# Zero-padded QK matmuls in 128x32 tiles, and an output projection spread over eight steps, in an attention + SwiGLU block

## The chip, the cores and the metric

The kernel runs on one core of one Trainium2 chip. The metric is the device time of one execution in microseconds (us), and the table values are medians of several executions. Executions of one kernel agreed within about 0.6%. A ratio is computed as the mean time of one kernel's runs over the mean time of the other's runs of the same rounds, so it is not quite the ratio of the medians quoted beside it. "The profile" is one traced execution.

Names used below: PE is TensorE's matmul row, PEld its weight loads, ACT is ScalarE, DVE is VectorE, POOL is GpSimd, SP is SyncE. A *pass* is 512 columns streamed through the array; matmuls that sit in different tiles of the array and stream together share a pass. A *key tile* is 128 keys; a *step* is one query chunk of 512 tokens and one group of four heads, and has 16 key tiles. Attention has 32 steps, so 512 key tiles.

## The reference

S = 2048 tokens, D = 1024, 32 heads of 32 with one shared key/value head, F = 3584, bfloat16.

```python
mod = (silu(c) @ w_mod)                      # six vectors: sa, ca, ga, sb, cb, gb
h = layernorm(x) * (1 + ca) + sa
q, k, v = h @ wq, h @ wk, h @ wv             # 32 query heads, one k and one v of width 32
p = softmax(q @ k.T * 32 ** -0.5)
x = x + ga * ((p @ v) @ wo)
h = layernorm(x) * (1 + cb) + sb
x = x + gb * ((silu(h @ w1) * (h @ w3)) @ w2)
```

## The kernel before

Three stages follow each other: a front end (modulation, layer norm, q, k, v), attention with the output projection, and the MLP. The change touches mostly attention. Keys are stored transposed four times over, once in each group of 32 partitions (`kT4`), so that each of four heads can use its own 32 rows of the array. One matmul contracts over 32 rows, and two such row tiles stream side by side:

```python
def qk_pair(pair, kt, idx, qc, hg):
    rows = (0, 1) if pair == 0 else (2, 3)
    a_exp.wait(t, idx)                                   # the exp has read these two PSUM banks
    for r in rows:
        ins = t.matmul(self.bank(r), self.kT4[32 * r:32 * r + 32, kt * 128:(kt + 1) * 128],
                       self.qT8[32 * r:32 * r + 32, hg, qc * 512:(qc + 1) * 512],
                       start=True, stop=True, tile_position=(32 * r, 0))
    p_qk.inc(ins)

def pv_all(kt, idx, bpv, bden):
    a_expA.wait(t, idx + 1); a_expB.wait(t, idx + 1)
    pts = (ptA[idx % 3], ptA[idx % 3], ptB[idx % 3], ptB[idx % 3])
    for j in range(4):                                   # 128x32 column tiles, all four side by side
        t.matmul(self.bank(bpv)[32 * j:32 * (j + 1), :], self.V16[:, kt, :], pts[j][...],
                 start=(kt == 0), stop=(kt == NKT - 1), tile_position=(0, 32 * j))
    for j in range(4):                                   # the same with a block of ones: denominators
        ins = t.matmul(self.bank(bden)[32 * j:32 * (j + 1), :], self.ones_k[:, :], pts[j][...], ...)
    p_pv.inc(ins)
# ... per key tile: qk_pair(0, kt), qk_pair(1, kt), pv_all(kt - 1)
# ... only in the step with hg == 0: the projection of the previous query chunk, 64 matmuls of 128x128
```

ACT turns the scores into exps, one instruction for each pair of banks:

```python
p_qkA.wait(a, idx + 1)
a_expA.inc(a.activation(ptA[idx % 3][:], self.bank(0, 2), ACT.Exp, scale=scale))
p_qkB.wait(a, idx + 1)
a_expB.inc(a.activation(ptB[idx % 3][:], self.bank(2, 2), ACT.Exp, scale=scale))
```

At the end of a step DVE takes the reciprocal of the denominators and multiplies, both straight from PSUM; two pairs of banks alternate for PV and denominators, and the projection borrows the idle pair.

The softmax here doesn't subtract the row's maximum and nothing guards it: scores larger than these inputs give would overflow.

## Time and profile before

| | before |
|---|---|
| median | 1916.1 us (4 runs, 1915.8 to 1916.6) |
| first exp | 167.0 us |
| attention, first exp to the end of the last | 1092.0 us |
| from there to the MLP's first transpose | 30.2 us |
| MLP | 624.7 us |

The lines of the page: first the busy time of the engines as a share of the span, then rows of the 40 slices. In those rows a digit is the busy share in tenths, and in PEclk the granted share of the TensorE clock.

```profile
PE 1754.7 (92%) x9864; PEld 520.4 (27%) x9864; DVE 474.6 (25%) x698; ACT 1051.9 (55%) x1144; POOL 31.8 (2%) x43
...
PE   1797999999999999999999999969998998998999
...
ACT  0004999998988888888889999931100100110110
...
PEclk9897555558555558555567555568999999999999
```

The PE row says that PE is busy nearly everywhere. The PEclk row says that through the whole of attention this busy PE runs at half speed, apart from short rises (at 449, 722 and 995 us). At half clock a pass takes 0.43 us instead of 0.22 and counts as busy all the while, so the first row alone hides this. The Trainium skill distrusts that row for another reason: "Trainium Kernel Development and Optimization", section Performance Expectations, says that matmul busy time is a bad metric for how close a kernel is to the hardware's limit because matmuls are pipelined. It does not name the clock; here the row misleads because of the clock (97% busy at clock 0.50 in the first window below).

The windows view, three stretches: attention without projection, attention with it, and MLP. Columns are the stretch, its length, then busy us and number of instructions for each engine, the granted clock, the DMA share and GB/s.

```profile
core 0: us, PE busy (x) PEld busy (x) DVE busy (x) ACT busy (x) POOL busy (x), PEclk, DMA share, GB/s
205.00:405.00 200.00, 194.25 (x1142) 32.67 (x1140) 21.71 (x13) 183.04 (x190) 0.00 (x0) 0.50 0.00 1
449.00:475.00 26.00, 24.45 (x192) 7.35 (x188) 5.52 (x9) 21.55 (x24) 0.00 (x0) 1.00 0.00 1
1300.00:1500.00 200.00, 194.01 (x911) 88.11 (x910) 67.76 (x102) 24.48 (x41) 8.83 (x10) 0.99 0.32 106
```

Count the exps: 190 ACT instructions in 200 us is one in 1.053 us, so about 2.1 us for a key tile (2.107 us from the steps, which take 33.71 us for 16 key tiles). The groups of instructions (operation, shapes, count, busy us, mean ns of one, idle time before it and who ended it):

```profile
L474 PE MATMUL ps<-qT,kT 32*128 32x512 bf16 x2048 | 542.3, 584 | 62.2 <-ACT ptB L461 43.5
L459 ACT ACTIVATE ptA<-ps 128x1024 bf16<-128x1024 f32 x512 | 525.3, 1026 | 115.0 <-PE ps L474 109.3
L461 ACT ACTIVATE ptB<-ps 128x1024 bf16<-128x1024 f32 x512 | 521.6, 1019 | 0.0
```

ACT waits for QK before the A exp, 109.3 us in all. The timeline shows one such loop (start, length, engine, line, operation; in brackets the idle time before it and what ended it):

```profile
350.31 1.02 ACT L459 ACTIVATE ptA<-ps 128x1024 bf16<-128x1024 f32 x1 [0.24 <-PE ps L474]
...
350.67 0.61 PE L485 MATMUL ps<-ptA,V 128*32 128x512 bf16 x2
...
351.07 0.63 PE L491 MATMUL ps<-ptA,ones_k 128*32 128x512 bf16 x2
...
351.23 1.02 ACT L461 ACTIVATE ptB<-ps 128x1024 bf16<-128x1024 f32 x1
...
351.64 1.27 PE L474 MATMUL ps<-qT,kT 32*128 32x512 bf16 x4
352.30 0.10 PEld L474 LDWEIGHTS ps<-qT,kT 32*128 32x128 bf16 x2 [0.56 <-ACT ptB L461]
352.35 1.02 ACT L459 ACTIVATE ptA<-ps 128x1024 bf16<-128x1024 f32 x1
...
352.84 0.61 PE L485 MATMUL ps<-ptA,V 128*32 128x512 bf16 x2
```

The A exp at 350.31 is followed by the B exp 0.92 us later: that is ACT's own pace (0.919 us on average over the 646 intervals below 0.96 us). The PE needs 0.40 us from PV to the denominators and 0.57 us from there to the next QK; the matmuls come back to PV after 2.17 us here, 2.107 us on average. ACT could do a key tile in 1.84 us, so PE at half clock sets the pace.

### The profile page before, as it was taken

To read this page: it belongs to the slowest core of one execution; us is meant where nothing else is said; L and a number is where in the kernel's file an instruction comes from. 1 tells how busy PE (TensorE), PEld (TensorE's weight loads), DVE (VectorE), ACT (ScalarE), POOL (GpSimd) and SP (SyncE) were. 2 spreads that over 40 slices of the span, in tenths; PEclk is the share of its full clock that TensorE was granted. 3 is DMA by queue.
4 is the path that set the end of the run, shared out by engine and by line. 5 is a ranking of instruction groups with operands and counts; after the bars stand their busy time and mean duration, and the time that the engine had idled before them with its cause. 6 is when DMAs were issued, how large, how long until landed. Compare 5 with 4: busy or idle time off the path is not lost. (4 is left out here: it accounts for less than half of the span.)

```text
span 1913.9 us, 23304 instructions
## 1 busy us (share of the span) xinstructions
PE 1754.7 (92%) x9864; PEld 520.4 (27%) x9864; DVE 474.6 (25%) x698; ACT 1051.9 (55%) x1144; POOL 31.8 (2%) x43
## 2 busy tenths in 40 slices
PE   1797999999999999999999999969998998998999
PEld 0342111112111112111121111124444444444444
DVE  5551100102501013010112101133413423332431
ACT  0004999998988888888889999931100100110110
POOL 1000000000000000000000000000000000000000
PEclk9897555558555558555567555568999999999999
DMA  9305100000000000000000000002412512421420
GB/s 319 132 1 187 56 1 1 1 1 1 1 1 1 1 1 1 1 1 1 1 1 1 1 1 1 1 1 88 154 38 96 175 56 66 165 94 61 132 89 22
DMA packets 48293, 93.30 MB, mean 49 GB/s; under 512 B 1392, under 2 KB 30064, under 8 KB 48192
## 3 DMA queue, kind: packets, MB, share of 16 engines
q1 hardware_dynamic: 39360, 57.94, 8.9%
q0 software_dynamic: 8832, 33.88, 5.2%
q8 instruction: 79, 1.29, 0.3%
q14 instruction: 22, 0.18, 0.0%
HBM read 87.62 MB, written 4.19 MB: 48 GB/s over the span
## 5 line engine op out<-in xcount | busy, mean ns | idle before, releaser
L474 PE MATMUL ps<-qT,kT 32*128 32x512 bf16 x2048 | 542.3, 584 | 62.2 <-ACT ptB L461 43.5
L459 ACT ACTIVATE ptA<-ps 128x1024 bf16<-128x1024 f32 x512 | 525.3, 1026 | 115.0 <-PE ps L474 109.3
L461 ACT ACTIVATE ptB<-ps 128x1024 bf16<-128x1024 f32 x512 | 521.6, 1019 | 0.0
L673 ACT ACTIVATE sg<-ps 128x512 bf16<-128x512 f32 x112 | 66.9, 597 | 504.1 <-PE ps L743 504.1
L579 DVE RECIPROCAL rden<-ps 128x512 f32<-128x512 f32 x32 | 107.3, 3352 | 841.6 <-PE ps L491 841.6
L491 PE MATMUL ps<-ptA,ones_k 128*32 128x512 bf16 x1024 | 313.5, 611 | 0.0
L491 PE MATMUL ps<-ptB,ones_k 128*32 128x512 bf16 x1024 | 313.5, 611 | 0.0
L485 PE MATMUL ps<-ptA,V 128*32 128x512 bf16 x1024 | 302.4, 588 | 0.8 <-ACT ptB L461 0.8
L485 PE MATMUL ps<-ptB,V 128*32 128x512 bf16 x1024 | 302.4, 588 | 0.0
L474 PEld LDWEIGHTS ps<-qT,kT 32*128 32x128 bf16 x2048 | 103.2, 98 | 661.9 <-ACT ptA L459 377.8
L743 PE MATMUL ps<-h2T,w1b 128*128 128x512 bf16 x896 | 218.0, 387 | 15.2 <-DVE h2T L695 15.2
L748 PE MATMUL ps<-h2T,w3b 128*128 128x512 bf16 x896 | 213.5, 381 | 0.0
L761 PE MATMUL ps<-w_sb,hact 128*128 128x512 bf16 x896 | 194.1, 379 | 3.4 <-DVE hact L707 3.4
L703 DVE TENSOR_TENSOR gs<-ps,sg 128x512 bf16<-128x512 f32 x112 | 77.4, 691 | 190.1 <-ACT sg L673 190.1
L743 PEld LDWEIGHTS ps<-h2T,w1b 128*128 128x128 bf16 x896 | 88.7, 99 | 124.6 <-DVE h2T L695 16.0
L748 PEld LDWEIGHTS ps<-h2T,w3b 128*128 128x128 bf16 x896 | 88.3, 99 | 107.9 <-issue 3.9
L761 PEld LDWEIGHTS ps<-w_sb,hact 128*128 128x128 bf16 x896 | 87.4, 98 | 110.1 <-DVE hact L707 5.3
L485 PEld LDWEIGHTS ps<-ptA,V 128*32 128x32 bf16 x1024 | 52.5, 100 | 215.4 <-issue 215.4
L707 DVE TENSOR_TENSOR hact<-ps,gs 128x512 bf16<-128x512 f32 x112 | 77.4, 691 | 53.9 <-PE ps L748 53.9
L459 ACT ACT_TABLE_LOAD x1 | 1.3, 1283 | 135.8 <-PEq L126 135.8
L511 PE MATMUL ps<-wo_sb,oT 128*128 128x512 bf16 x256 | 67.5, 408 | 4.3 <-DVE oT L582 4.3
L714 DVE TENSOR_TENSOR x_sb<-ps,x_sb 128x512 bf16<-128x512 f32 x32 | 22.1, 691 | 175.1 <-PE ps L761 175.1
(69 smaller groups left out, 616.4 us busy)
## 6 DMA issues: line engine op xcount, KB each, us to landing
w1b<-in_B_w_dram SPq DMA_DIRECT2D x28, 1024.0 KB, 5.3
w3b<-in_B_w_dram POOLq DMA_DIRECT2D x28, 1024.0 KB, 8.0
wmod_sb<-in_w_mod_dram SPq DMA_DIRECT2D x2, 6144.0 KB, 27.7
w_sb<-in_B_w_dram SPq DMA_DIRECT2D x1, 7168.0 KB, 29.3
x_sb<-in_A_x_dram SPq DMA_DIRECT2D x4, 1024.0 KB, 10.5
out_dram<-x_sb SPq DMA_DIRECT2D x16, 256.0 KB, 2.0
wq_sb<-in_A_wq_dram POOLq DMA_DIRECT2D x1, 2048.0 KB, 18.1
wo_sb<-in_A_wo_dram POOLq DMA_DIRECT2D x1, 2048.0 KB, 23.9
```

The costliest lines, as they stand in the source:

```text
L459: a_expA.inc(a.activation(ptA[idx % 3][:], self.bank(0, 2), ACT.Exp, scale=scale))
L461: a_expB.inc(a.activation(ptB[idx % 3][:], self.bank(2, 2), ACT.Exp, scale=scale))
L474: ins = t.matmul(self.bank(r), self.kT4[32 * r:32 * r + 32, kt * 128:(kt + 1) * 128], self.qT8[32 * r:32 * r + 32, hg, qc * 512:(qc + 1) * ...
L485: t.matmul(self.bank(bpv)[32 * j:32 * (j + 1), :], self.V16[:, kt, :], pts[j][:, jj * 512:(jj + 1) * 512], start=(kt == 0), stop=(kt == NK ...
L491: ins = t.matmul(self.bank(bden)[32 * j:32 * (j + 1), :], self.ones_k[:, :], pts[j][:, jj * 512:(jj + 1) * 512], start=(kt == 0), stop=(kt ...
L511: ins = t.matmul(self.bank(bnk), self.oT[:, hg2, j * 128:(j + 1) * 128], self.wo_sb[:, hg2, half * 512:(half + 1) * 512], start=(hg2 == 0) ...
L579: c0 = v_r.inc(v.reciprocal(self.rden[:], self.bank(bden)))
L703: v_gs.inc(v.tensor_tensor(self.gs[k][:], self.bank(4 + 2 * k), self.sg[k][:], op=ALU.mult))
L707: v_hact.inc(v.tensor_tensor(self.hact[:, fc, :], self.bank(5 + 2 * k), self.gs[k][:], op=ALU.mult))
L743: ins = t.matmul(self.bank(4 + 2 * k), self.w1b[buf][:, cch, sub * 128:(sub + 1) * 128], self.h2T[b][:, cch, :], start=(cch == 0), stop=(c ...
L748: ins = t.matmul(self.bank(5 + 2 * k), self.w3b[buf][:, cch, sub * 128:(sub + 1) * 128], self.h2T[b][:, cch, :], start=(cch == 0), stop=(c ...
L761: ins = t.matmul(self.bank(bnk), self.hact[:, fc, j * 128:(j + 1) * 128], self.w2_sb[:, fc, half * 512:(half + 1) * 512], start=(fc == 0), ...
```

## The change

The intent is to give the array more work on purpose, so that the clock gate opens (the throttle that sets PE's granted clock, in these traces always 0.50 or 1.00): QK now contracts over all 128 rows, with three quarters of the stationary operand zero, in the same 128x32 tiling that PV uses. Around it, the projection is spread over all eight steps of a query chunk, PV and denominators are copied out of PSUM early so that one pair of banks is enough, the front end's loads are reordered, and w1/w3 blocks are halved and no longer prefetched (the padded keys need the memory). The core of the diff, with cuts:

```diff
-                self.kT4 = ER12(nc.sbuf_tensor("kT4", [P, S], BF16, side="right"))
+                self.kTpad = ER12(nc.sbuf_tensor("kTpad", [P, 4, S], BF16, side="right"))
 ...  POOL zeroes it once; DVE writes head r's keys to its own 32 partitions of copy r
+                SM["g_pad"].inc(g.memset(self.kTpad[:], 0.0))
+                            ins3 = v.tensor_copy(self.kTpad[32 * r:32 * r + 32, r, qc * 512:(qc + 1) * 512],
+                                                 self.bank(BK)[32 * r:32 * r + 32, :])
 ...  QK
-                        ins = t.matmul(self.bank(r), self.kT4[32 * r:32 * r + 32, kt * 128:(kt + 1) * 128],
-                                       self.qT8[32 * r:32 * r + 32, hg, qc * 512:(qc + 1) * 512],
-                                       start=True, stop=True, tile_position=(32 * r, 0))
+                        for c in range(4):
+                            k0 = kt * 128 + 32 * c
+                            ins = t.matmul(self.bank(r)[32 * c:32 * (c + 1), :], self.kTpad[:, r, k0:k0 + 32],
+                                           self.qT8[:, hg, qc * 512:(qc + 1) * 512],
+                                           start=True, stop=True, tile_position=(0, 32 * c))
 ...  projection: 64 units of four 128x32 matmuls, eight units in each step, one per key tile
-                    op_chunks = oproj_chunks(qc - 1) if (hg == 0 and qc > 0) else []
+                    if hg == 0 and qc > 0:
+                        units = oproj_units(qc - 1)
+                    my_units = units[8 * hg:8 * hg + 8] if units else []
 ...  end of a step on DVE
-                        c0 = v_r.inc(v.reciprocal(self.rden[:], self.bank(bden)))
+                        v_evac.inc(v.tensor_copy(self.pv_sb[:], self.bank(bpv)))
+                        v_evac.inc(v.tensor_copy(self.den_sb[:], self.bank(bden)))
+                        v_evac.wait(v, v_evac.count)
+                        c0 = v_r.inc(v.reciprocal(self.rden[:], self.den_sb[:]))
 ...  front end: modulation weights before most of x; wq, wk, wv, wo released by them
-                for i in range(4):
+                d_x[0].inc(sp.dma_start(self.x_sb[:, 0:TPC, :], self.xv[:, 0:TPC, :]), 16)
+                d_wm[0].inc(sp.dma_start(wmod_sb[:], wmod_v[:, :, 0:HALF]), 16)
+                for i in range(1, 4):
                     d_x[i].inc(sp.dma_start(self.x_sb[:, i * TPC:(i + 1) * TPC, :], ...), 16)
-                d_wm[0].inc(sp.dma_start(wmod_sb[:], wmod_v[:, :, 0:HALF]), 16)
-                d_x[3].wait(g, 16)
+                d_wm[0].wait(g, 16)
 ...  MLP blocks of 256 columns, allocated after attention
-            NPRE = min(2, self.NQC * self.FB)
+            NPRE = 0
```

More of the change, by code (lines that the diff above doesn't have):

```diff
@@ L60, in __init__ @@
         DH = D // H
-        assert DH == 32 and D % P == 0 and S % 512 == 0 and F % 512 == 0
+        assert DH == 32 and D % P == 0 and S % 512 == 0 and F % 256 == 0
         assert tuple(w_mod.shape) == (D, 6 * D)
@@ L69, in __init__ @@
         self.FC = F // P
-        self.FB = F // 512
+        self.FW = 256
+        self.FPB = self.FW // P
+        self.FB = F // self.FW
         assert self.HG == self.DC
@@ L82, in build @@
                 "d_c", "d_x0", "d_x1", "d_x2", "d_x3", "d_wmod", "d_wmod2", "d_wo", "d_wqkv", "d_w2", "d_w1a", "d_w1b", "d_w3a", "d_w3b", "o_out",
-                "g_aux",
+                "g_aux", "g_pad",
                 "a_sig", "a_sd", "a_expA", "a_expB", "a_sg",
@@ L87, in build @@
                 "v_aux", "v_mod", "v_wo", "v_st", "v_xn", "v_ht", "v_kev", "v_vev", "v_qev",
-                "v_r", "v_evac", "v_res", "v_gs", "v_hact", "v_w2s",
+                "v_r", "v_evac", "v_ot", "v_res", "v_gs", "v_hact", "v_w2s",
             ]
@@ L133, in build @@
                 self.w2_sb = EL2(nc.sbuf_tensor("w2_sb", [P, FC, D], BF16))
-                self.w1b = [EL2(nc.sbuf_tensor(f"w1b{i}", [P, DC, 512], BF16)) for i in range(2)]
-                self.w3b = [EL2(nc.sbuf_tensor(f"w3b{i}", [P, DC, 512], BF16)) for i in range(2)]
                 with ExitStack() as stR2:
@@ L140, in build @@
                     self.rden = ER2(nc.sbuf_tensor("rden", [P, 512], F32, side="right"))
-                    self.oT = ER2(nc.sbuf_tensor("oT", [P, HG, 512], BF16, side="right"))
+                    self.pv_sb = ER2(nc.sbuf_tensor("pv_sb", [P, 512], F32, side="right"))
+                    self.den_sb = ER2(nc.sbuf_tensor("den_sb", [P, 512], F32, side="right"))
+                    self.oT = ER2(nc.sbuf_tensor("oT", [P, 2, HG, 512], BF16, side="right"))
                     self.phase2()
@@ L145, in build @@
                     ER3 = stR3.enter_context
+                    self.w1b = [ER3(nc.sbuf_tensor(f"w1b{i}", [P, DC, self.FW], BF16, side="right")) for i in range(2)]
+                    self.w3b = [ER3(nc.sbuf_tensor(f"w3b{i}", [P, DC, self.FW], BF16, side="right")) for i in range(2)]
                     self.xn2 = ER3(nc.sbuf_tensor("xn2", [P, 4, D], BF16, side="right"))
@@ L355, in _ @@
                     p_k.wait(v, qc + 1)
-                    v_kev.inc(v.tensor_copy(self.kT4[:, qc * 512:(qc + 1) * 512], self.bank(BK)))
                     p_v.wait(v, qc + 1)
@@ L363, in _ @@
                         v_qev.inc(v.tensor_copy(self.qT8[:, hg, qc * 512:(qc + 1) * 512], self.bank(bq)))
+                        if 2 <= hg < 6:
+                            if qc == 0 and hg == 2:
+                                SM["g_pad"].wait(v, 1)
+                            r = hg - 2
+                            ins3 = v.tensor_copy(self.kTpad[32 * r:32 * r + 32, r, qc * 512:(qc + 1) * 512],
+                                                 self.bank(BK)[32 * r:32 * r + 32, :])
+                            if r == 3:
+                                v_kev.inc(ins3)
                     if qc == 0:
@@ L428, in _ @@
                         v_kev.wait(sp, v_kev.count)
-                        o.inc(sp.dma_start(dbg["kT4"], self.kT4[:]), 16)
+                        o.inc(sp.dma_start(dbg["kT4"], self.kTpad[:]), 16)
                     if "V16" in dbg:
@@ L487, in pv_all @@
                                  start=(kt == 0), stop=(kt == NKT - 1), tile_position=(0, 32 * j))
+                    if kt == 0:
+                        v_evac.wait(t, 2 * (idx // NKT))
                     ins = None
@@ L494, in pv_all, with oproj_units @@
                     p_pv.inc(ins)
-                def oproj_chunks(qc):
-                    chunks = []
+                v_ot = SM["v_ot"]
+                def oproj_units(qc):
+                    ob = qc % 2
+                    units = []
                     for g in range(8):
@@ L500, in oproj_chunks, with emit @@
                         bnk = BOP + g % 2
-                        def grp(g=g, j=j, half=half, bnk=bnk, first=True):
-                            pass
-                        for c2 in range(2):
-                            def emit(g=g, j=j, half=half, bnk=bnk, c2=c2):
-                                if c2 == 0:
+                        for hg2 in range(HG):
+                            def emit(g=g, j=j, half=half, bnk=bnk, ob=ob, hg2=hg2):
+                                if hg2 == 0:
                                     v_res.wait(t, 8 * qc + g - 2 + 1)
@@ L507, in emit @@
                                     if g == 0:
-                                        v_evac.wait(t, (qc + 1) * HG)
+                                        v_ot.wait(t, (qc + 1) * HG)
                                 ins = None
-                                for hg2 in range(4 * c2, 4 * c2 + 4):
-                                    ins = t.matmul(self.bank(bnk), self.oT[:, hg2, j * 128:(j + 1) * 128],
+                                for cq in range(4):
+                                    ins = t.matmul(self.bank(bnk)[32 * cq:32 * (cq + 1), :],
+                                                   self.oT[:, ob, hg2, j * 128 + 32 * cq:j * 128 + 32 * (cq + 1)],
@@ L512, in emit @@
                                                    self.wo_sb[:, hg2, half * 512:(half + 1) * 512],
-                                                   start=(hg2 == 0), stop=(hg2 == HG - 1))
-                                if c2 == 1:
+                                                   start=(hg2 == 0), stop=(hg2 == HG - 1), tile_position=(0, 32 * cq))
+                                if hg2 == HG - 1:
                                     p_op.inc(ins)
-                            chunks.append(emit)
@@ L517, in oproj_chunks @@
-                    return chunks
+                            units.append(emit)
+                    return units
                 NSTEP = NQC * HG
+                bpv, bden = 4, 5
                 qk_pair(0, 0, 0, 0, 0)
                 qk_pair(1, 0, 0, 0, 0)
+                units = []
                 for step in range(NSTEP):
                     qc, hg = step // HG, step % HG
-                    s = step % 2
-                    bpv, bden = 4 + 2 * s, 5 + 2 * s
                     base = step * NKT
-                    op_chunks = oproj_chunks(qc - 1) if (hg == 0 and qc > 0) else []
@@ L528, in _ @@
-                    v_evac.wait(t, step - 1)
-                    if s == 1 and hg == 1 and qc > 0:
-                        v_res.wait(t, 8 * qc)
-                    n_op = len(op_chunks)
+                    if hg == 0 and qc > 0:
+                        units = oproj_units(qc - 1)
+                    my_units = units[8 * hg:8 * hg + 8] if units else []
+                    kt0 = 4 if NKT >= 12 else 1
+                    upk = (8 + (NKT - kt0 - 1)) // (NKT - kt0)
                     for kt in range(1, NKT):
@@ L535, in _ @@
                         qk_pair(1, kt, idx, qc, hg)
+                        if kt == 1:
+                            v_evac.wait(t, 2 * step - 1)
                         pv_all(kt - 1, idx - 1, bpv, bden)
-                        if op_chunks and kt >= 3:
-                            k_issue = 2 if len(op_chunks) > (NKT - 1 - kt) else 1
-                            for _ in range(k_issue):
-                                if op_chunks:
-                                    op_chunks.pop(0)()
+                        if kt >= kt0:
+                            for _ in range(upk):
+                                if my_units:
+                                    my_units.pop(0)()
                     if step + 1 < NSTEP:
@@ L546, in _ @@
                     pv_all(NKT - 1, base + NKT - 1, bpv, bden)
-                    while op_chunks:
-                        op_chunks.pop(0)()
-                for emit in oproj_chunks(NQC - 1):
+                    while my_units:
+                        my_units.pop(0)()
+                for emit in oproj_units(NQC - 1):
                     emit()
@@ L553, in _, with residual @@
             def _(v):
-                def residual(qc):
-                    for g in range(8):
+                v_ot = SM["v_ot"]
+                res_done = {}
+                def residual(qc, upto):
+                    done = res_done.get(qc, 0)
+                    for g in range(done, min(8, upto)):
                         j, half = g // 2, g % 2
@@ L561, in residual @@
                                                   self.x_sb[:, tok, half * 512:(half + 1) * 512], op=ALU.add))
-                    v_res.wait(v, v_res.count)
-                    self.ln_stats(v, range(4 * qc, 4 * qc + 4))
+                    new_done = max(done, min(8, upto))
+                    res_done[qc] = new_done
+                    if new_done == 8 and done < 8:
+                        v_res.wait(v, v_res.count)
+                        self.ln_stats(v, range(4 * qc, 4 * qc + 4))
                 v_w2s = SM["v_w2s"]
+                bpv, bden = 4, 5
                 for qc in range(NQC):
@@ L568, in _ @@
                         step = qc * HG + hg
-                        s = step % 2
-                        bpv, bden = 4 + 2 * s, 5 + 2 * s
-                        if hg == 0 and qc > 0:
-                            residual(qc - 1)
                         if step == min(HG + 1, NQC * HG - 1):
@@ L578, in _ @@
                         p_pv.wait(v, (step + 1) * NKT)
-                        c0 = v_r.inc(v.reciprocal(self.rden[:], self.bank(bden)))
+                        v_evac.inc(v.tensor_copy(self.pv_sb[:], self.bank(bpv)))
+                        v_evac.inc(v.tensor_copy(self.den_sb[:], self.bank(bden)))
+                        v_evac.wait(v, v_evac.count)
+                        c0 = v_r.inc(v.reciprocal(self.rden[:], self.den_sb[:]))
                         v_r.wait(v, c0)
-                        p_op.wait(v, 8 * qc)
-                        v_evac.inc(v.tensor_tensor(self.oT[:, hg, :], self.bank(bpv), self.rden[:], op=ALU.mult))
-                        v_evac.wait(v, v_evac.count)
-                residual(NQC - 1)
+                        p_op.wait(v, 8 * (qc - 1))
+                        v_ot.inc(v.tensor_tensor(self.oT[:, qc % 2, hg, :], self.pv_sb[:], self.rden[:],
+                                                 op=ALU.mult))
+                        v_ot.wait(v, v_ot.count)
+                        if qc > 0:
+                            residual(qc - 1, hg + 1)
+                residual(NQC - 1, 8)
             d_w1 = [SM["d_w1a"], SM["d_w1b"]]
@@ L596, in _ @@
                 d_w2.inc(sp.dma_start(self.w2_sb[:], w2_v), 16)
+                FW = self.FW
                 for gfb in range(NPRE):
                     fb = gfb % self.FB
-                    d_w1[gfb % 2].inc(sp.dma_start(self.w1b[gfb % 2][:], w1_v[:, :, fb * 512:(fb + 1) * 512]), 16)
+                    d_w1[gfb % 2].inc(sp.dma_start(self.w1b[gfb % 2][:], w1_v[:, :, fb * FW:(fb + 1) * FW]), 16)
                 if "x_att" in dbg:
@@ L607, in _ @@
             def _(g):
+                FW = self.FW
                 for gfb in range(NPRE):
                     fb = gfb % self.FB
-                    d_w3[gfb % 2].inc(g.dma_start(self.w3b[gfb % 2][:], w3_v[:, :, fb * 512:(fb + 1) * 512]), 16)
+                    d_w3[gfb % 2].inc(g.dma_start(self.w3b[gfb % 2][:], w3_v[:, :, fb * FW:(fb + 1) * FW]), 16)
     def phase3(self):
@@ L614, in phase3 @@
         S, D, F, DC, NT, NQC, FC, FB = self.S, self.D, self.F, self.DC, self.NT, self.NQC, self.FC, self.FB
+        FW, FPB = self.FW, self.FPB
         dbg = self.dbg
@@ L644, in _ @@
                         if gfb >= self.n_w13_prefetched:
-                            p_up.wait(sp, 4 * (gfb - 1))
-                            d_w1[buf].inc(sp.dma_start(self.w1b[buf][:], w1_v[:, :, fb * 512:(fb + 1) * 512]), 16)
+                            p_up.wait(sp, FPB * (gfb - 1))
+                            d_w1[buf].inc(sp.dma_start(self.w1b[buf][:], w1_v[:, :, fb * FW:(fb + 1) * FW]), 16)
                     for j in range(4):
@@ L659, in _ @@
                         if gfb >= self.n_w13_prefetched:
-                            p_up.wait(g, 4 * (gfb - 1))
-                            d_w3[buf].inc(g.dma_start(self.w3b[buf][:], w3_v[:, :, fb * 512:(fb + 1) * 512]), 16)
+                            p_up.wait(g, FPB * (gfb - 1))
+                            d_w3[buf].inc(g.dma_start(self.w3b[buf][:], w3_v[:, :, fb * FW:(fb + 1) * FW]), 16)
             @blk.scalar
@@ L733, in _ @@
                         k = gfc % 2
-                        fb = fc // 4
+                        fb = fc // FPB
                         gfb = tc * FB + fb
                         buf = gfb % 2
-                        sub = fc % 4
+                        sub = fc % FPB
                         d_w1[buf].wait(t, 16 * (gfb // 2 + 1))
```

## The prediction

> **What bounds the kernel now.** The windows table shows three stages: front end to 166 us, attention 167 to 1259 us (1092 us), then tail and MLP to 1914 us. The MLP has PE 97% busy at clock 0.99. In attention PE looks 95% busy and ACT 89%, but the granted clock is 0.50 outside the four steps that carry the output projection. In the timeline one key tile takes 2.107 us there: two QK passes (32-row tiles, two at a time) and two PV/ones passes of 0.43 us each, plus switches of tiling; ACT idles 0.30 to 0.54 us between pairs of exps. Where ACT is not held up, exps start every 0.919 us. So attention is bound by the half-speed PE in a loop with ACT; its ACT floor is 1024 x 0.919 = 941 us.
>
> **Why the clock is low.** Streamed columns times array area come to 31% of full-speed PE per 3.41 us window in attention, and the clock stays 0.5; windows with output projection (44 to 50%, nearly all that half speed can do) are followed by 1.0, which 34 to 38% held for a while. The Trainium skill, "TensorE: Matmul & The Clock Gate", Part 1, says that activity releases the throttle in windows of about 3.4 us; the clock records here change in multiples of 3.41 us.
>
> **What the change does.**
> 1. QK becomes 16 zero-padded 128x32 matmuls per key tile instead of four 32x128: four passes, not two. At half clock six passes need 6 x 0.427 = 2.56 us, a dense PE, so the clock should rise within three windows. At full clock they take 6 x 0.22 = 1.3 us of 1.84 us (70% area, well above what held the clock). All attention matmuls share one tiling; the skill, "TensorEngine Tiling (Array Packing)", Key Properties, says a change of mode drains the array: QK to PV is 0.317 us at full clock, PV to ones 0.226.
> 2. Loop at full clock: exp end, +0.06, two passes 0.61, +0.10: next exp at 1.78 us against ACT's 1.84. ACT becomes the bound, barely. Projection units, now spread over eight steps, cost an estimated 0.05 us x 192 = 9 us; warm-up 2 us. Attention: about 952 us, saving 140.
> 3. Earlier modulation weights: front end saves about 4 us. Extra K copies hide under 1.73 us PE groups.
> 4. Two PSUM copies (0.69 us each) before the last reciprocal, late layer-norm statistics: +2 to 3 us.
> 5. w1/w3 blocks are halved and not prefetched: the first loads (about 5 us) hide behind transposes and h2T (7.4 us). In steady state a 1 MB pair must land in 6.9 us; 2 MB took 8.0 to 8.3 of 13.8 us. My estimate is 6.5 us: tight, about +8 us of stalls.
>
> **Prediction.** 1916 - 140 - 4 + 3 + 8, about 1780 us; 1760 to 1812 in 8 of 10. Faster by over 2%: 0.94; within 2%: 0.02; slower: 0.04.
>
> **What would show it.** Clock near 1.0 across attention; exps every 0.92 us; 1.84 to 1.88 us per key tile; PE busy share falling there, ACT nearly 100%; QK passes 0.22 us apart; MLP gate matmuls waiting little for w3b.
>
> **What would make it wrong.** If zero-padded work did not count as activity, the clock would stay 0.5, a key tile would take 2.6 us and the kernel about 2160 us. If starting 16 matmuls after a wait costs over 0.06 us, ACT idles each time: 0.1 us a tile is 51 us. If 512-byte rows land slower, each 0.5 us is 26 us.

## The result, and the profile after

The changed kernel takes 1771.5 us (8 runs, 1769.7 to 1774.3) against 1916.8 us in the same rounds, ratio 0.9244, 95% interval 0.9235 to 0.9253.

| stage, us in the trace | before | after | difference | predicted |
|---|---|---|---|---|
| front end, to the first exp | 167.0 | 157.6 | -9.4 | -4 |
| attention | 1092.0 | 953.5 | -138.5 | -140 |
| to the MLP's first transpose | 30.2 | 32.6 | +2.4 | +3 |
| MLP | 624.7 | 626.7 | +2.0 | +8 |
| span | 1913.9 | 1770.3 | -143.6 | -133 |

The same rows of the page, after:

```profile
PE 1537.3 (87%) x16776; PEld 596.5 (34%) x16776; DVE 523.7 (30%) x774; ACT 1024.5 (58%) x1144; POOL 63.4 (4%) x72
...
PE   2797888888888888888888888599989999998999
...
ACT  0004999999999999999999999111001101100110
...
PEclk9899999999999999999999999799999999999999
```

PE has 70% more matmuls (16776 against 9864) and is busy for 217 us less; the clock is full in all of attention, and ACT is at 9 tenths throughout. The windows (steps without projection, steps with it, MLP; columns as before):

```profile
190.00:390.00 200.00, 167.11 (x2616) 49.45 (x2616) 36.61 (x27) 199.86 (x219) 0.00 (x0) 1.00 0.01 2
400.00:600.00 200.00, 173.07 (x2796) 57.84 (x2792) 53.33 (x59) 199.13 (x215) 0.00 (x0) 1.00 0.01 2
1150.00:1350.00 200.00, 192.85 (x891) 86.75 (x892) 65.96 (x101) 23.63 (x40) 16.77 (x19) 0.97 0.36 106
```

ACT is busy for 199.86 of 200 us: it is the bound now. The first step takes 30.4 us while the clock rises, the other steps without projection 29.33 us (1.833 us a key tile), those with it mostly 29.86.

```profile
L489 PE MATMUL ps<-qT,kTpad 128*32 128x512 bf16 x8192 | 629.6, 385 | 141.8 <-ACT ptB L474 121.4
L472 ACT ACTIVATE ptA<-ps 128x1024 bf16<-128x1024 f32 x512 | 532.7, 1041 | 4.0 <-PE ps L489 0.9
L474 ACT ACTIVATE ptB<-ps 128x1024 bf16<-128x1024 f32 x512 | 530.6, 1036 | 0.0
```

ACT's wait for QK has gone from 109.3 to 0.9 us in the table; now PE waits for the exps (121.4 us). The loop in the timeline, a step without projection:

```profile
300.07 1.05 ACT L472 ACTIVATE ptA<-ps 128x1024 bf16<-128x1024 f32 x1
...
300.26 0.62 PE L489 MATMUL ps<-qT,kTpad 128*32 128x512 bf16 x8 [0.30 <-ACT ptB L474]
...
300.70 0.38 PE L500 MATMUL ps<-ptA,V 128*32 128x512 bf16 x2
...
300.92 0.38 PE L508 MATMUL ps<-ptA,ones_k 128*32 128x512 bf16 x2
...
300.99 1.05 ACT L474 ACTIVATE ptB<-ps 128x1024 bf16<-128x1024 f32 x1
...
301.18 0.61 PE L489 MATMUL ps<-qT,kTpad 128*32 128x512 bf16 x8
301.90 1.05 ACT L472 ACTIVATE ptA<-ps 128x1024 bf16<-128x1024 f32 x1
```

QK to PV takes 0.44 us, two passes of 0.22 with no switch of tiling, and the PE idles 0.30 us waiting for an exp. The A exps are 1.83 us apart.

### The profile page after: what moved, and what is told of

Read it like the earlier page. It is cut to its first block, busy times and chain, and to the rows that moved or that the text cites. A ratio compares the mean times of both kernels' runs of the same rounds, so it can differ in the third digit from the quotient of the medians.

```text
span 1770.3 us, 37227 instructions
## 1 busy us (share of the span) xinstructions
PE 1537.3 (87%) x16776; PEld 596.5 (34%) x16776; DVE 523.7 (30%) x774; ACT 1024.5 (58%) x1144; POOL 63.4 (4%) x72
## 5 line engine op out<-in xcount | busy, mean ns | idle before, releaser
L489 PE MATMUL ps<-qT,kTpad 128*32 128x512 bf16 x8192 | 629.6, 385 | 141.8 <-ACT ptB L474 121.4
L489 PEld LDWEIGHTS ps<-qT,kTpad 128*32 128x32 bf16 x8192 | 135.4, 94 | 556.4 <-ACT ptB L474 387.7
L603 DVE COPY pv_sb<-ps 128x512 f32<-128x512 f32 x32 | 22.1, 691 | 744.2 <-PE ps L508 744.2
L500 PE MATMUL ps<-ptA,V 128*32 128x512 bf16 x1024 | 196.0, 380 | 0.9 <-ACT ptB L474 0.9
L508 PE MATMUL ps<-ptA,ones_k 128*32 128x512 bf16 x1024 | 196.1, 380 | 0.0
L508 PE MATMUL ps<-ptB,ones_k 128*32 128x512 bf16 x1024 | 196.0, 380 | 0.0
L500 PE MATMUL ps<-ptB,V 128*32 128x512 bf16 x1024 | 196.0, 380 | 0.0
L606 DVE RECIPROCAL rden<-den_sb 128x512 f32<-128x512 f32 x32 | 107.3, 3353 | 1.1
L694 POOL DMA_DIRECT2D w3b<-in_B_w_dram x56 | 49.4, 883 | 1619.6 <-POOLq L459 1105.2
L529 PE MATMUL ps<-wo_sb,oT 128*32 128x512 bf16 x1024 | 90.8, 388 | 6.5 <-DVE oT L609 5.6
```

The source lines that it names most:

```text
L489: ins = t.matmul(self.bank(r)[32 * c:32 * (c + 1), :], self.kTpad[:, r, k0:k0 + 32], self.qT8[:, hg, qc * 512:(qc + 1) * 512], start=True, ...
L529: ins = t.matmul(self.bank(bnk)[32 * cq:32 * (cq + 1), :], self.oT[:, ob, hg2, j * 128 + 32 * cq:j * 128 + 32 * (cq + 1)], self.wo_sb[:, h ...
L606: c0 = v_r.inc(v.reciprocal(self.rden[:], self.den_sb[:]))
```

## The experiments

The main claim, that added work raises the clock, was to be told apart from these rivals: that uniform tiling (no switches between 32-row and 32-column tiles) did it; that the new PSUM handling and the spread projection did it; and, later, that the clock follows the time in which PE streams and not the area it fills. Below, "area" is worked out from the matmul records: columns streamed in a window of 3.41 us, each weighted with rows x columns of its tile / 16384, over the columns that a full-speed array could stream in that window. A full-speed pass is taken as 0.2135 us. This is an estimate from the clock of up to 2.4 GHz that the Trainium skill states ("TensorE: Matmul & The Clock Gate", table at the top), at which 512 columns take 0.2133 us; the traces show passes 0.216 us apart. "Time streamed" is the same sum with every pass counted as a full one, whatever the area of its tiles.

### e1_unpadded: the change without the padding

```diff
-    t.matmul(bank(r)[32*c:32*(c+1), :], kTpad[:, r, k0:k0+32], qT8[:, hg, ...], tile_position=(0, 32*c))   # x16
+    t.matmul(bank(r), kT4[32*r:32*r+32, kt*128:(kt+1)*128], qT8[32*r:32*r+32, hg, ...], tile_position=(32*r, 0))  # x4
```

> The changed kernel with only the QK matmuls put back: four 32x128 row tiles per key tile on unpadded keys. Everything else of the change stays (projection spread over eight steps, PV and denominators copied out of PSUM, new load order, halved weight blocks). Theory (the padded work raises the clock): the clock falls back to about 0.5 in attention, the eight steps without projection take about 33.7 us each as before, those with projection 34 to 37 us, the kernel about 1910 to 1950 us, so all of the attention gain is gone. Rival (the gain comes from the new PSUM handling and the spread projection): most of the 138 us stay, about 1790 to 1820 us. Rival (uniform tiling): gain gone as well, but then the padded kernel with mixed tiling must lose it too.

Measured: 1860.5 us (1854.6 to 1864.9), ratio 0.9706; attention 1042.6 us. Neither range was hit. The windows of the steps without projection and of steps with it:

```profile
200.00:390.00 190.00, 185.34 (x1084) 31.63 (x1082) 27.47 (x22) 173.76 (x181) 0.00 (x0) 0.50 0.00 1
520.00:680.00 160.00, 143.20 (x1106) 31.18 (x1106) 30.13 (x25) 149.38 (x159) 0.00 (x0) 0.71 0.00 1
```

The first eight steps are those of the kernel before to within 0.04 us (33.71 us, clock 0.50). So without padding the clock does not rise there, as the theory said. But with the spread projection the clock is 0.71: the records show it at 1.0 for some 14 us and at 0.5 for some 17 us in turn. I had not seen that the spread units also feed the clock. The trace shows the units of a step bunched in its key tiles 4 to 11, so for half a step a key tile has four passes' worth of area (0.405 at half clock) and for the other half three (0.30): in the step from 463.9 to 495.8 us the units run from 473.8 to 487.0 us, and the clock is 1.0 from 475.8 to 492.9 us. Of the 138.5 us of attention, 49 remain without the padding.

### e2_pad128: the same padded work in another tiling

```diff
-    for c in range(4): t.matmul(bank(r)[32*c:32*(c+1), :], kTpad[:, r, k0:k0+32], ..., tile_position=(0, 32*c))
+    t.matmul(bank(r), kTpad[:, r, kt*128:(kt+1)*128], ...)          # one 128x128 matmul per head
```

> The changed kernel with the same zero-padded QK work, but as four full 128x128 matmuls per key tile instead of sixteen 128x32: the same four passes, but the tiling now changes twice per key tile. Theory (activity sets the clock): clock stays near 1.0 in attention; two changes of tiling cost an estimated 0.03 to 0.06 us per key tile because PE has slack, so 1771 to 1800 us. Rival (uniform tiling is what gained): back to near 1900 us, or at least half of the 138 us lost.

Measured: 1809.0 us (1808.2 to 1812.7), ratio 0.9443; attention 990.1 us, clock 1.00 in the windows. The timeline of one key tile:

```profile
300.00 0.61 PE L487 MATMUL ps<-qT,kTpad 128*128 128x512 bf16 x2 [0.17 <-ACT ptB L474]
...
300.53 0.39 PE L498 MATMUL ps<-ptA,V 128*32 128x512 bf16 x2
...
300.76 0.38 PE L506 MATMUL ps<-ptA,ones_k 128*32 128x512 bf16 x2
...
301.08 0.61 PE L487 MATMUL ps<-qT,kTpad 128*128 128x512 bf16 x2
```

QK to PV is 0.53 us instead of 0.44, and denominators to QK 0.32: each change of tiling costs about 0.09 us. The clock does not need uniform tiling, so that rival is out as the cause of the clock. But uniform tiling is worth 37 us of attention here (990.1 against 953.5), and the kernel is 9 us over the 1800 at most that I had allowed. My reading is that a key tile with six passes leaves the loop little slack (30.24 us a step without projection instead of 29.33, 31.11 with it instead of 29.86).

### e3_dummy: useless work added to the kernel before

```diff
+    t.matmul(self.bank(rows[0]), self.ident[:], self.qT8[:, hg, qc * 512:(qc + 1) * 512], start=True, stop=True)
     for r in rows:
         ins = t.matmul(self.bank(r), self.kT4[32 * r:32 * r + 32, ...], ...)     # overwrites it
```

> The kernel before, with one useless 128x128 matmul (512 columns, stationary operand the identity) added ahead of each QK pair, into a PSUM bank that the QK matmul then overwrites: two extra full passes per key tile, nothing else changed. Theory: the extra activity raises the clock to near 1.0, and the kernel with more work gets faster: key tile about 1.95 to 2.0 us against 2.107, kernel about 1840 to 1870 us. Rival (the clock does not follow such work, or the gain is elsewhere): clock 0.5, about 3.0 us per key tile, about 2350 to 2450 us.

Measured: 2033.1 us (2032.0 to 2034.4), ratio 1.0609: slower, and in neither range. The windows show why:

```profile
200.00:550.00 350.00, 336.77 (x1540) 61.33 (x1566) 28.34 (x14) 228.71 (x224) 0.00 (x0) 0.50 0.00 1
650.00:830.00 180.00, 165.02 (x1240) 44.88 (x1260) 23.77 (x12) 172.32 (x181) 0.00 (x0) 1.00 0.00 1
```

Both halves of the expectation came true, one after the other. For eight steps the clock stays at 0.50 and a key tile takes 3.13 us. Then the step with the projection raises the clock, and it stays at 1.0 to the end of attention: a key tile takes 1.997 us, so with more work and mixed tiling those steps are faster (31.95 us) than those of the kernel before (33.71 us). The same code thus has two stable speeds. The area explains both. At half clock the key tile has four passes of full and two of half area, 5 x 0.2135 / 3.133 = 0.34; at full clock the same work in less time gives 5 x 0.2135 / 1.997 = 0.53.

Putting the windows of the six traces so far together gave a rule: area of 0.375 or more in one window, clock 1.0 in the next; less, 0.5. It fails in 15 of 3246 windows. A rule by the time streamed, with its best threshold (0.435), fails in 56. Useless work counts as area: with the identity matmuls left out, e3 at full clock would have 3 x 0.2135 / 1.997 = 0.32, and it held the clock for 799 us. The identity has no empty rows, so e3 does not say whether zero rows count; e5 does. All of this was fitted to traces already seen. The runs e5 and e6 test the rule where the two measures disagree.

### e4_order: the front end's load order alone

```diff
+    d_x[0] ...                     # first x chunk
     d_wm[0] ...                    # modulation weights, first half
-    (all four x chunks before it)
+    d_x[1], d_x[2], d_x[3] ...
-    d_x[3].wait(g, 16)
+    d_wm[0].wait(g, 16)
```

> The kernel before with only the front end's load order changed as in the change (first x chunk, then the first half of the modulation weights, then the other x chunks; wq and wo released by the modulation weights). The trace of the changed kernel has its first exp 9.5 us earlier than before, of which I had expected 4. Theory: the order alone gives all of it, 1906 to 1908 us against 1916. Rival (the padded memset and key copies or the PE clock in the front end changed it): 1911 us or more.

Measured: 1907.1 us (1906.9 to 1909.9), ratio 0.9956 (0.9943 to 0.9970); first exp at 158.0 us instead of 167.0. The order alone gives 9.0 of the front end's 9.4 us.

### e5_row64: half the padding, in two passes

```diff
-    for r in rows: for c in range(4): t.matmul(bank(r)[32*c:32*(c+1), :], kTpad[:, r, k0:k0+32], ...)
+    for b, r in enumerate((0, 2) if pair == 0 else (1, 3)):
+        t0 = 64 * (r // 2)
+        ins = t.matmul(self.bank(2 * pair + b), self.kTpad[t0:t0 + 64, r, kt * 128:(kt + 1) * 128],
+                       self.qT8[t0:t0 + 64, hg, ...], tile_position=(t0, 0))
```

PV takes its operands in the new order of heads.

> The changed kernel with QK as four 64x128 row tiles per key tile, heads 0 and 2 side by side, then 1 and 3: padded to 64 rows instead of 128. Two QK passes as in the kernel before (PE streams for as long), but each fills the whole array. From the six traces so far I read a rule: in a 3.41 us window, streamed columns times array area (rows x columns of the tile, zero rows counted) at or above 0.375 of a full-speed array is followed by clock 1.0, below it by 0.5 (15 of 3246 windows disagree; time streamed, whatever the area, does worse: 56). Theory (area counts): at half clock 4 passes x 0.2135 / 2.107 = 0.405, above 0.375, so the clock is 1.0 from the first few key tiles on, and at 1.0 it is 0.46, so it stays. With two passes less than the change, steps with projection come down from 29.86 to about 29.4 us: 1755 to 1762 us, faster than the change. Rival (time streamed counts, not area): the streaming is that of the kernel with unpadded QK, so clock 0.5 in the first eight steps, about 1850 us.

Measured: 1761.4 us (1757.6 to 1761.9), ratio 0.9183; attention 939.3 us.

```profile
200.00:390.00 190.00, 135.50 (x1246) 32.75 (x1246) 32.00 (x24) 190.00 (x209) 0.00 (x0) 1.00 0.00 1
520.00:680.00 160.00, 121.56 (x1234) 32.69 (x1234) 35.64 (x38) 160.00 (x176) 0.00 (x0) 1.00 0.00 1
```

PE streams two QK passes per key tile, like the kernel without padding, but the clock is 1.0 from the first few key tiles on. ACT is busy in every moment of both windows (its records overlap here; around 300 us the exps start 0.917 us apart), and all steps take 29.13 to 29.63 us, with and without projection. Mixed tiling costs nothing visible here, with four passes in a key tile. Filled area decides, not time streamed, and zero rows count: without them e5 would have, at half clock, the 0.30 of the kernel before, which stayed at 0.5.

### e6_half64: just around the threshold

```diff
-    t0 = 64 * (r // 2)                                   # as e5, 64 rows for all heads
+    n = 64 if pair == 0 else 32                          # heads 0 and 2: 64 rows; heads 1 and 3: 32
+    t0 = n * (32 * r // n)
```

> As e5_row64, but only heads 0 and 2 are padded to 64 rows, heads 1 and 3 stay at 32. Theory (area, threshold 0.375): at half clock 3.5 passes give 0.355, just below, with windows spread by some 0.05 around it, and at 1.0 0.41, just above: so in the first eight steps the clock goes up within some 10 to 40 us and then mostly stays at 1.0, with some windows of 0.5; with projection units (0.40 at half, 0.46 at full) it stays at 1.0. About 1760 to 1785 us. Rival (time streamed): about 1850 us with clock about 0.7 as for unpadded QK.

Measured: 1776.0 us (1772.1 to 1778.2), ratio 0.9267; attention 954.6 us in the trace. The clock is 0.89 between 200 and 390 us and 0.96 between 520 and 680 us, so the time lies in the expected range and the clock was mostly at 1.0, but with projection units it still dropped now and then, which I had not expected. Six windows of one clock decision each:

```profile
184.70:188.10 3.40, 2.63 (x26) 0.62 (x24) 0.00 (x0) 3.27 (x5) 0.00 (x0) 1.00 0.00 0
188.10:191.50 3.40, 2.35 (x24) 0.61 (x22) 1.68 (x3) 3.40 (x5) 0.00 (x0) 1.00 0.00 0
191.60:195.00 3.40, 2.35 (x24) 0.56 (x24) 3.37 (x2) 3.40 (x5) 0.00 (x0) 1.00 0.02 7
195.00:198.40 3.40, 2.35 (x28) 0.62 (x24) 0.19 (x1) 3.40 (x5) 0.00 (x0) 1.00 0.00 0
198.40:201.80 3.40, 3.40 (x22) 0.45 (x15) 0.00 (x0) 3.23 (x4) 0.00 (x0) 0.50 0.00 0
201.80:205.20 3.40, 2.62 (x26) 0.62 (x24) 0.00 (x0) 3.24 (x5) 0.00 (x0) 1.00 0.00 0
```

The areas that I work out for these windows are 0.44, 0.38, 0.41, 0.37, 0.38, 0.44: the fourth falls below 0.375 and the fifth window is at half clock. It also shows that "PE busy" is highest, 3.40 of 3.40 us, in the one window at half clock, although the area done there (0.38) lies within the range of the others. In this run the rule fails most often (13 of 510 windows): some windows of 0.35 to 0.37 at half clock are still followed by 1.0, so the threshold is good to about 0.02, not to three digits.

### e7_padonly and e9_row64only: padding alone in the kernel before

For e7 the sixteen padded matmuls replace QK in the kernel before; the w1/w3 buffers had to move behind attention for want of memory. For e9 the 64-row tiles of e5 do (with its order of heads in PV), with two zero-padded copies of the keys, and everything else, prefetch included, stays.

```diff
-    self.kT4 [P, S];  v_kev.inc(v.tensor_copy(self.kT4[:, ...], self.bank(BK)))
+    self.kTpad [P, 4, S] (e7) or [P, 2, S] (e9), zeroed by POOL, filled 32 partitions at a time
     QK as in the change (e7) or as in e5 (e9)
```

> The kernel before with the padded sixteen 128x32 QK matmuls alone; projection still bunched into one step in eight, two PV bank pairs, old load order; the w1/w3 buffers (512 columns) are allocated after attention for want of memory, so not prefetched. Theory (the padded work raises the clock; the spread only removes a few us): steps without projection 29.3 us, the three with projection about 38 to 41 us, attention about 970 to 980 us instead of 1092, kernel about 1795 to 1805 us. Rival (the change needs its spread projection for the clock, as the unpadded run with spread projection at clock 0.71 might suggest): clock falls to 0.5 in steps without projection, over 1900 us.

> The kernel before with only QK changed, to the 64-row padded tiles of e5_row64 (keys in two zero-padded copies); prefetch, projection, PSUM banks and load order as before. Theory (area counts): clock 1.0 in all of attention, steps without projection 29.4 us, the three with it 36 to 38 us, attention 964 to 972 us, kernel 1788 to 1798 us. Rival (time streamed counts): clock 0.5 except around the projection, about 1910 us as before.

Measured: e7 1798.6 us (1796.7 to 1801.0), ratio 0.9382, attention 973.2 us; e9 1787.6 us (1787.1 to 1788.8), ratio 0.9325, attention 961.5 us. e7 lies within its ranges, e9 is just faster than its own. Both clocks are 1.0 in attention; e7's windows, then e9's:

```profile
200.00:390.00 190.00, 159.37 (x2484) 47.09 (x2480) 24.81 (x13) 189.86 (x207) 0.00 (x0) 1.00 0.01 2
520.00:680.00 160.00, 138.56 (x2028) 43.06 (x2032) 24.87 (x17) 151.69 (x165) 0.00 (x0) 1.00 0.01 2
...
200.00:390.00 190.00, 135.63 (x1246) 32.48 (x1246) 28.35 (x14) 190.00 (x209) 0.00 (x0) 1.00 0.01 4
520.00:680.00 160.00, 121.61 (x1066) 30.98 (x1066) 25.09 (x17) 154.20 (x168) 0.00 (x0) 1.00 0.00 1
```

e9 is the closest pair to the kernel before: the same number of QK matmuls and passes, and the clock goes from 0.50 to 1.00 with the zero rows alone. Padding alone (e7) takes 119 of the 138.5 us off attention. What the spread projection adds on top is arithmetic: bunched, three steps take 39.86 instead of 29.39 us (+31.4 us in all); spread, 24 steps take 0.53 us longer each (+12.7). The difference, 18.7 us, is close to the 19.7 us between e7's attention and that of the change. In e9 the bunched steps take 36.97 us.

### e10_after_again and e11_row64_again: the change and its 64-row version on one chip

> The changed kernel again, unaltered, on one chip with the next run, since the 64-row version was so far compared with it only across chips (1761.4 against 1771.5 us, each with its own runs of before). Expected 1771 us, ratio 0.924.

> The 64-row version of the changed kernel again, on the same chip. If it is really faster: 1759 to 1763 us, ratio 0.918, 0.5 to 0.7 per cent below the changed kernel. If the difference was between chips: within 0.2 per cent of it.

Measured: the change 1774.0 us (1770.4 to 1775.6), ratio 0.9254 (0.9241 to 0.9266); the 64-row version 1759.8 us (1756.6 to 1762.5), ratio 0.9178 (0.9166 to 0.9191). The 64-row version is 0.8% faster than the change, a little more than expected, all of it in attention (939.3 against 953.4 us), and the fastest kernel.

### The versions side by side

| version | area at half clock, without projection | attention, us | median, us |
|---|---|---|---|
| before | 3 x 0.2135 / 2.107 = 0.30 | 1092.0 | 1916 |
| e4, load order alone | the same | 1092.1 | 1907 |
| e1, change without padding | the same | 1042.6 | 1861 |
| e3, before + useless passes | 0.34 | 1209.0 | 2033 |
| e2, change with padded 128x128 | dense | 990.1 | 1809 |
| e7, padding alone | dense | 973.2 | 1799 |
| e9, 64-row QK alone | 0.405 | 961.5 | 1788 |
| e6, 64 rows for half the heads | 0.355 | 954.6 | 1776 |
| the change | dense, 0.50 | 953.5 | 1772 and 1774 |
| e5, the change with 64 rows | 0.405 | 939.3 | 1761 and 1760 |

## Why the prediction was right, point by point

**The bound before and the cause of the low clock: right, and sharper now.** The prediction read from the kernel before that about 31% of the array per window kept the clock at 0.5, and that projection windows raised it. It did not have the rule, and it counted four steps with projection where attention has three. The Trainium skill ("TensorE: Matmul & The Clock Gate", Part 1) says that the gate is set "based on how busy the PE has been recently", in windows of about 3.4 us; the clock records agree on the window. But PE was 97% busy by the profile in the window from 205 to 405 us (194.25 of 200) and stayed at half clock. What counts, as far as these runs show, is columns times tile area, with zero rows included and with a threshold near 0.375 of the full-speed array (0.30 stayed at half clock, 0.405 rose within 5 us, 0.355 went up and down).

**Step 1, more passes raise the clock within three windows: right.** The clock was 1.0 from 162 us on, 5 us after the first exp. The area at full clock was about 0.70 without projection, as predicted.

**Step 2, ACT becomes the bound, attention 952 us: right.** It took 953.5. Steps without projection took 29.33 us, a key tile 1.833 us, and ACT's wait for QK fell to 0.9 us; the estimated slack of 0.06 us in the loop held. The projection units cost 24 x 0.53 = 12.7 us against an estimate of 9. Warm-up was about 1 us, not 2. That the sum came within 1.5 us is partly luck: the steps' floor was 32 x 29.33 = 938.6 us, 2.4 less than the predicted 941, and made up for most of the dearer projection.

**What the prediction did not separate.** It gave the whole gain of attention to the clock and named the shared tiling only in passing. The runs split it differently. Padding in 128x128 form, with the clock at 1.0 just the same, loses 37 us, so uniform tiling mattered too, most likely because six passes leave little slack. And the spread projection lifts the clock without any padding, to about 0.71 (e1), which both of my ranges for that run missed. The shares depend on the order in which one adds the parts: padding is worth 119 us alone and 89 us on top of the rest (1042.6 - 953.5).

**Step 3, front end: the mechanism right, the size off.** I predicted -4 and measured -9.4. The term that was mis-sized is, by my own working, the landing of the later x chunks: I took the layer-norm statistics to end at about 46 us and they ended at 41.8 us (those of the last chunk began at 36.5). e4 shows that the order alone gives -9.

**Step 4, end of attention: right,** +2.4 us against +2 to 3. This was read from the trace, not tested by a run.

**Step 5, weight loads of the MLP: too pessimistic.** I expected 8 us of stalls from 1 MB pairs landing in 6.5 of 6.9 us. The w3 blocks landed in 5.7 us (median) and no matmul of the MLP is listed as waiting for a DMA. What the 2.0 us are that the MLP lost stays open. It spends 29.4 us at half clock instead of 27.4, but that is not enough: e6, with the same weight blocks and only 23.1 us at half clock, has an MLP of 625.6 us, still 0.9 us over that of the kernel before.

**Off by 8.5 us in the median** (1780 against 1771.5), and by 10.6 us in the trace (-133 against -143.6): the front end was 5.4, the MLP 6.0 and the end 0.6 us better than predicted, attention 1.5 us worse.

**What stays open.** The rule is worked out from matmul records and clock records. No run shows what the hardware counts; a few per cent of matmul records can be missing from a trace, and near the threshold the rule fails in some windows (13 of 510 in e6). In all these kernels a pass fills all 128 columns of the array, so the runs do not tell rows times columns from rows alone. Whether weight loads or transposes count was not tested.

## What to carry to other kernels

Read the granted clock beside PE's busy share before believing that PE is full: at half clock a pass takes 0.43 us instead of 0.22 and counts as busy all the while, which hides the loss. If a loop of small-row matmuls sits below the threshold (here 0.30), filling the idle rows with zeros can take the clock from 0.50 to 1.00 for everything on PE (e9); pad by just enough (64 rows here, area 0.405) that the loop keeps its slack, since each extra pass and each change of tiling then comes out of that slack. Check the level at half clock as well as at full clock: e3 had two stable speeds with the same code, and only the projection's burst brought it from one to the other.

## What the Trainium skill lacked or had wrong

- "TensorE: Matmul & The Clock Gate", Part 1: says that busy-ness opens the gate, not how it is measured. Here a PE that the profile shows 97% busy stays at 0.5 (before, 205 to 405 us), and columns x tile area of at least about 0.375 of the full-speed array in one 3.41 us window foretells clock 1.0 in the next (wrong in 15 of 3246 windows of six traces; time streamed, whatever the area, in 56).
- The same page, "Why this matters for your kernels", row on small-K matmuls: advises 32-row tiles for their concurrency and does not say that passes which fill only half of the rows can leave the clock at half (here 0.50). Here 64-row tiles with zeros, with as many passes, brought attention from 1092.0 to 961.5 us (e9).
- The same page, Part 1: lacks that the gate gives one program two stable speeds. With identical code e3 ran 3.13 us a key tile at 0.5 and 1.997 us at 1.0.
- "TensorEngine Tiling (Array Packing)", Key Properties: says that a change of mode drains the array, without a figure. Here it cost about 0.09 us per change at full clock (e2: 0.53 us against 0.44 from QK to PV).
- No page read says why the recorded length of one and the same ACT instruction varies: around 300 us in e5 the exps are recorded with 1.28 us each, in the kernel before with 1.02, while in both they can start 0.92 us apart. That the longer record includes waiting behind the instruction before it is a reading that no run here tests.
